# Two first products, then two second products: a reordered main stage in a three-layer kernel on one Trainium2 core

## The chip, the cores and the metric

One core of a Trainium2 chip runs the whole program. TensorE (PE) multiplies matrices, with its weight loads shown apart (PEld); VectorE (DVE), ScalarE (ACT) and GpSimd (POOL) do elementwise work; SyncE (SP) issues the transfers. The metric is the device time of one execution in microseconds, the median of three runs: 2111.48 us for the kernel before (2109.56 to 2112.36).

## The reference

Three layers on 4 x 576 = 2304 tokens of width 512. All values are float32.

```
x = attention(q, k, v, ...)                       # local softmax attention and a memory term
P = sinkhorn(exp(x @ w_gate))                     # 2304 x 8, a weight per token and expert
out = 0
for e in range(8):                                # the experts
    h = max(x @ w1[e], 0)                         # 512 -> 1024
    out += P[:, e:e+1] * (h @ w2[e])              # 1024 -> 512
h = out @ w_in                                    # the wide layer: 512 -> 2048
y = max(0.01*h, h) @ w_out                        # 2048 -> 512
```

## The kernel before

Attention, the gate and the first expert take the first 424 us. All later work is in `rest`, and the change is in its loop over `steps`. Every float32 operand there is split into a high and a low part, and a product is three matmuls: high by high, low by high, high by low.

**Steps.** The tokens go through in two passes, 1280 tokens and 1024. A pass has token groups `s`: two of 512 tokens (`s` = 0, 1), and in the first pass a third of 256 (`s` = 2). A unit `u` is 512 hidden columns: experts 1 to 7 are units 2 to 15, the wide layer is units 16 to 19. A unit's columns come in two halves, `fp` = 0 and 1. The segments are: experts on the first pass (84 steps), experts on the second (56), the wide layer on the first (24) and on the second (16). The order is unit, group, half.

**One step.** `l1(st)` computes the half's hidden values: 42 matmuls of 256 columns into four PSUM banks `pq` (a Strassen-like scheme of seven products, `PRODUCTS`), or 24 into one bank for `s` = 2. After the first bank, ACT copies a part of it (`s`, L918) and six DVE operations (L920 to L925) put the sums into `c`; then `half(0)` and `half(1)` each make the high part `hh` on ACT (L931) and the low part `hl` on DVE (L932). `l2(st)` multiplies `hh` and `hl` by the second weights into four banks `po`: 24 matmuls of 512 columns, the last of them cut into two of 256 (12 for `s` = 2). After the second half, DVE adds `po` times the token's weight to `acc` (L971).

**Pipeline.** Each turn of the loop calls `l1` of step k and then `l2` of step k-1, so PE alternates first and second products. `tc.manual_schedule()` keeps each engine's instructions in the order of the code.

**Work on the side.** In `l1`, right after the copy `s`, `pay()` calls `W.advance()` and one turn of a generator `side`:

- `W` stages weights into three slots; step (u, fp) uses instance number `inst`, and slot `inst % 3`. Each instance has two stages. Stage 0 splits the first half of `w1` (ACT copies, then POOL subtractions, L677) and makes sums on POOL (L689 to L692). Stage 1 splits those sums, the operand `s` of four of the seven products, and then `w2`. A stage may run when the products that read the slot's old content have been issued; `W.finish(inst)` at the head of `l1` runs on the spot what is missing of its instance.
- `side` builds operands for later segments: loads, ACT copies, POOL subtractions (`stl`, L735, and four sums L740 to L743).
- `conv.advance(n)` turns the wide layer's float64 weights into float32 in steps: two DVE operations a step (L804 to L813), then one POOL addition `wb` (L814) per piece.

`put_by` holds back the stores of a finished group's `acc` to the next turn.

Of the kernel before, what the change touches and what calls it, by code (L numbers as in the profile page):

```python
# [15 lines left out]
AF = mybir.ActivationFunctionType  # L16
# [4 lines left out]
P = 128  # L21
B, H, S, D = 4, 8, 576, 64
NT, DM, E, F, G = 2304, 512, 8, 1024, 2048
# [621 lines left out]
SB = 256  # L645
# [3 lines left out]
class Pairs:  # L649
# [23 lines left out]
    keep = staticmethod(lambda one: one)  # L673
# [149 lines left out]
def rest(tc, pools, W, X, xd, Pm, ident, keep, out, conv):  # L823
# [3 lines left out]
    nc = tc.nc  # L827
# [4 lines left out]
    acc = [ap.tile([P, DM], F32, name=f"acc{t}") for t in range(10)]  # L832
    kept = {(seg, s): {part: dr.tile([P, 7 * 2 * SB], F32, name=f"k{part}{seg}{s}") for part in "hl"} for seg in (1, 2, 3) for s in range(2)}
    segs = [dict(n=n, bases=PASSES[n % 2], units=range(2, 16) if n < 2 else range(16, 20)) for n in range(4)]
    steps = []
# [10 lines left out]
    def tiles(st):  # L846

        seg, s = st[0], st[2]
        T = SB if s == 2 else 2 * SB
        return T, range(4 * s, 4 * s + T // P), seg["bases"][0] // P  # L850
# [97 lines left out]
    def l2(st):  # L948
        seg, u, s, fp, inst = st
        w = W.finish(inst)  # L950
        hh, hl = hs.pop(st[1:])
        T, ts, t0 = tiles(st)
        banks = (2, 3, 0, 1) if s == 1 and fp == 1 and 2 in range(len(seg["bases"])) else tuple(range(T // P)) if s < 2 else (2, 3)
        if fp == 0:
            for j in banks:
                po[j] = pp.tile([P, DM], F32, tag=f"po{j}", name=f"po{j}")
        for f in range(2):
            for j in banks:
                r = slice(j % (T // P) * P, (j % (T // P) + 1) * P)
                for n, (a, part) in enumerate(((hh, "h"), (hh, "l"), (hl, "h"))):  # L960
                    for d in (slice(0, SB), slice(SB, DM)) if f and n == 2 and j == banks[-1] else (slice(0, DM),):
                        nc.tensor.matmul(po[j][:, d], a[:, f, r], w[1, part][:, f, d], start=(fp == 0 and f == 0 and n == 0), stop=(fp == 1 and f == 1 and n == 2 and d.stop == DM))  # L962
        if last_of[inst] is st:
            W.gone.add((inst, 1))
        if fp == 0:
            return
        e = u // 2
        for j in banks:
            t = ts[j % len(ts)]
            if u < 16:  # L970
                nc.vector.scalar_tensor_tensor(out=acc[t], in0=po[j], scalar=Pm[:, t0 + t, e:e + 1], in1=acc[t], op0=ALU.mult, op1=ALU.add)  # L971
            elif u == 16:
                nc.scalar.activation(acc[t], po[j], AF.Copy)
            else:
                nc.vector.tensor_add(acc[t], po[j], acc[t])
            if u == 19:
                nc.sync.dma_start(out=out[(t0 + t) * P:(t0 + t + 1) * P, :], in_=acc[t])
# [17 lines left out]
    def plain_from_x():  # L995
        xs = from_dram(nc, ap, xd, PASSES[0][2], P)
        at_tail["x"] = True
        yield
        for n, x in enumerate(xs):
            r = slice(n * P, (n + 1) * P)  # L1000
            nc.scalar.activation(xp["h"][:, :, r], x, AF.Copy)
            nc.vector.tensor_sub(xp["l"][:, :, r], x, f32(xp["h"][:, :, r]))
        yield

    def second_half():

        for s, t0 in enumerate(PASSES[1]):
            for n in range(2):
                xa, xb = from_dram(nc, ap, xd, t0 + n * P, SB)
                yield  # L1010
                yield from staged(1, s, n, xa, xb)
# [15 lines left out]
    def next_layer(n):  # L1027

        t0 = PASSES[n][0] // P
        rounds = [(s, j) for s in range(2) for j in range(2)]  # L1030
        of = [(t0 + 4 * s + j, t0 + 4 * s + 2 + j) for s, j in rounds]
        if n == 0:
            of.append((t0 + 8, t0 + 9))
        ts = loaded(*of.pop(0))
        yield
        at_tail["x"] = True
        yield
        for s, j in rounds:
            xs = []
            for k, a in enumerate(ts):  # L1040
                x = ap.tile([P, 4, P], F32, tag=f"x{'ab'[k]}", name=f"x{'ab'[k]}", bufs=1)
                nc.scalar.activation(x, turned(a), AF.Copy)
                xs.append(x)
            yield
            ts = loaded(*of.pop(0)) if of else ()
            for k, _ in enumerate(staged(n + 2, s, j, *xs)):
                if k == 2:
                    if n == 0:
                        yield
                    if of or ts:  # L1050
                        at_tail["x"] = True
                yield
        if n == 0:
            for k, a in enumerate(ts):
                r = slice(k * P, (k + 1) * P)
                ps = turned(a)
                nc.scalar.activation(xp["h"][:, :, r], ps, AF.Copy)
                nc.vector.tensor_sub(xp["l"][:, :, r], ps, f32(xp["h"][:, :, r]))
            yield

    def side(n):

        if n == 0:
            yield from plain_from_x()
            yield from second_half()
        elif n < 3:
            yield
            yield
            yield from next_layer(n - 1)

    more = owed = None
    at_tail = {}
    sides = []
    put_by = []
    for k, st in enumerate(steps):
        seg, u, s, fp, inst = st
        if more is None or seg is not steps[k - 1][0]:
            more = side(seg["n"])
            sides.append(more)
        for t in put_by:  # L1080
            nc.sync.dma_start(out=keep[t * P:(t + 1) * P, :], in_=acc[t - seg_t0])
        put_by = []
        last_half = l1(st)
        turn = [more]
        last = steps[k - 1] if k else None
        behind = k and (last[2] == 2 and last[3] == 1 or u >= 16)
        if last_half and not behind:
            last_half()
        if k:
            l2(last)  # L1090
            if behind and at_tail.pop("x", None):
                next(turn.pop(), None)
            if last_half and behind:
                last_half()
            if last[1] == 15 and last[3] == 1:
                _, ts, seg_t0 = tiles(last)
                put_by = [seg_t0 + t for t in ts]
        if u == 2 and fp == 1:
            _, ts, t0 = tiles(st)
            for t in ts:  # L1100
                nc.scalar.activation(acc[t], acc[t], AF.Copy, scale=Pm[:, t0 + t, 0:1])
        if at_tail.pop("x", None):
            next(turn.pop(), None)
        owed = turn
        if seg["n"] < 2:
            conv.advance(1 + (k % 2 if seg["n"] == 0 else 1))
    l2(steps[-1])
    assert all(next(one, None) is None for one in sides) and next(conv.todo, None) is None

# [4 lines left out]
def body(tc, qt, kt, qn, vn, zn, beta, M_prev, w_gate, w1, w2, w_in, w_out, out):  # L1114
    nc = tc.nc
    with ExitStack() as ctx:
# [138 lines left out]
        with right, ExitStack() as rx:  # L1255
            pool = lambda name, bufs=1, **kw: rx.enter_context(tc.tile_pool(name=name, bufs=bufs, reuse_waits="tile", **kw))
            ap, hp_, conv_ = pool("r_acc"), pool("r_h"), pool("r_conv")
            pq, pp = pool("r_pq", 4, space=PSUM), pool("r_po", space=PSUM)
            conv = Convert(tc, conv_, w_in, w_out, *wide)
            with tc.manual_schedule():  # L1260
                rest(tc, (ap, hp_, pq, pp, dr), WR, X, xd, Pm, ident, keep, out, conv)
# [39 lines left out]
```

## Time and profile before

| | |
|---|---|
| median of three runs | 2111.48 us |
| profiled execution, its own time | 2110.44 us |
| its span in the trace | 2108.6 us |
| PE busy | 2091.1 us, 99% of the span |
| DVE, POOL, ACT busy | 66%, 53%, 36% |
| chain that ended last: PE | 94% |
| granted TensorE clock | 1.0 throughout |

The span is the traced execution from its first to its last instruction. The chain that ended last follows the program back from its last instruction to what released each one. PE's line numbers are L911 (first products), L897 (first products of `s` = 2) and L962 (second products).

### The profile page before, as it was taken

The numbers are of one execution on the slowest core, as the hardware profiler recorded it, in microseconds if no ns is written. First come the engines' busy times: TensorE is split into PE (matmuls) and PEld (weight loads), VectorE is DVE, ScalarE is ACT, GpSimd is POOL, SyncE is SP. The second block draws the span as 40 slices with busy tenths as digits, with TensorE's granted clock in tenths as the row PEclk, the third lists the DMA queues.
The fourth block names the chain that finished last, engine by engine and source line by source line (L and its number), as shares of the span: only waits on it lengthen the run. The fifth ranks groups of instructions, "written<-read, shape, count | busy, mean of one in ns | idle before, by whom it ended". The sixth has DMA issues, their size and how long they took to land.

```text
span 2108.6 us, 35243 instructions
## 1 busy us (share of the span) xinstructions
PE 2091.1 (99%) x13845; PEld 1853.6 (88%) x13845; DVE 1393.3 (66%) x2507; ACT 764.1 (36%) x1575; POOL 1116.9 (53%) x1011
## 2 busy tenths in 40 slices
PE   8899999999999999999999999999999999999999
PEld 5677778999999999999999999999999999999998
DVE  7766557366766666666666788666666665666676
ACT  7766643343332222222222433332323324333331
POOL 4522223556755444554444678775555554665651
PEclk9999999999999999999999999999999999999999
DMA  6544312354422222212227343421111161337111
GB/s 198 179 125 123 114 55 81 100 170 145 131 84 68 65 71 71 76 65 66 71 71 286 103 146 96 127 70 60 51 50 61 41 240 61 110 99 262 42 60 40
DMA packets 164422, 217.81 MB, mean 103 GB/s; under 512 B 13984, under 2 KB 109216, under 8 KB 162720
## 3 DMA queue, kind: packets, MB, share of 16 engines
q1 hardware_dynamic: 164256, 215.55, 31.7%
q8 instruction: 109, 1.79, 0.3%
q14 instruction: 57, 0.47, 0.1%
HBM read 166.23 MB, written 49.28 MB: 102 GB/s over the span
## 4 chain that ended last, share of the span: by engine, by line
PE 94%; DVE 2%; ACT 1%; POOL 1%; DMA 1%; issue 0%; SPq 0%; DVEq 0%; ACTq 0%; POOLq 0%
PE po L962 42%; PE pq L911 33%; PE pq L897 5%; PE ph L561 4%; PE po L569 4%; PE avps L313 2%; PE sps L252 1%; PE atps L287 1%; PE avps L310 1%; PE sps L246 1%; DVE a L263 1%; DMA nq<-in_qn_dram 1%; ACT a L265 1%; PE gps L410 0%; PE xt L1024 0%; DMA raw<-in_moe_w_dram 0%
## 5 line engine op out<-in xcount | busy, mean ns | idle before, releaser
L962 PE MATMUL po<-w,hh 128*128 128x512 f32 x2592 | 799.9, 390 | 0.0
L962 PEld LDWEIGHTS po<-w,hh 128*128 128x128 f32 x2592 | 473.3, 188 | 89.0
L962 PE MATMUL po<-w,hl 128*128 128x512 f32 (+1 forms) x1476 | 506.1, 363 | 0.0
L677 POOL TENSOR_TENSOR w0l<-raw,w0h 128x512 fp32r<-128x512 f32 x144 | 185.6, 1311 | 276.2 <-ACT w0h L676 276.2
L962 PEld LDWEIGHTS po<-w,hl 128*128 128x128 f32 x1476 | 276.9, 188 | 58.3
L932 DVE SCALAR_TENSOR_TENSOR hl<-c,hh 128x512 fp32r<-128x512 f32 x224 | 245.6, 1131 | 80.0 <-ACT hh L931 80.0
L911 PE MATMUL pq<-Xh,w0h 128*128 128x256 f32 x960 | 266.7, 278 | 0.0
L911 PE MATMUL pq<-Xl,w0h 128*128 128x256 f32 x960 | 265.7, 277 | 0.0
L911 PE MATMUL pq<-Xh,w0l 128*128 128x256 f32 x960 | 265.4, 276 | 0.0
L918 ACT ACTIVATE s<-pq 128x256 f32<-128x256 f32 x144 | 55.1, 383 | 489.9 <-PE pq L911 489.8
L677 POOL TENSOR_TENSOR w<-raw,w 128x512 fp32r<-128x512 f32 x144 | 217.6, 1533 | 0.0
L931 ACT ACTIVATE hh<-c 128x512 fp32r<-128x512 f32 x224 | 129.1, 624 | 232.0 <-DVE c L925 232.0
L971 DVE SCALAR_TENSOR_TENSOR acc<-po,Pm,acc 128x512 f32<-128x512 f32 x252 | 173.2, 740 | 29.7 <-PE po L962 28.4
L911 PEld LDWEIGHTS pq<-Xl,w0h 128*128 128x128 f32 x960 | 180.7, 188 | 0.0
L911 PEld LDWEIGHTS pq<-Xh,w0l 128*128 128x128 f32 x960 | 180.4, 188 | 0.0
L911 PEld LDWEIGHTS pq<-Xh,w0h 128*128 128x128 f32 x960 | 180.2, 188 | 0.0
L920 DVE TENSOR_TENSOR uv<-pq,s 128x256 f32<-128x256 f32 x144 | 60.7, 421 | 163.0 <-ACT s L918 162.8
L814 POOL TENSOR_TENSOR wb<-wa,wc 128x512 f32<-128x512 f32 x32 | 41.3, 1292 | 155.5 <-DVE wc L813 111.0
L677 POOL TENSOR_TENSOR ql<-raw,qh 128x512 fp32r<-128x512 f32 x48 | 62.3, 1319 | 90.2 <-ACT qh L676 90.2
L911 PE MATMUL pq<-Xh,w1h 128*128 128x256 f32 x384 | 106.1, 276 | 0.0
L911 PE MATMUL pq<-Xl,w1h 128*128 128x256 f32 x384 | 106.1, 276 | 0.0
L911 PE MATMUL pq<-Xh,w1l 128*128 128x256 f32 x384 | 106.1, 276 | 0.0
(266 smaller groups left out, 4842.5 us busy)
## 6 DMA issues: line engine op xcount, KB each, us to landing
raw<-in_moe_w_dram SPq DMA_DIRECT2D x136, 512.0 KB, 3.5
Xh<-kh SPq DMA_DIRECT2D x6, 1792.0 KB, 7.5
Xl<-kl SPq DMA_DIRECT2D x6, 1792.0 KB, 11.8
f<-in_moe_w_in_dram SPq DMA_DIRECT2D x16, 512.0 KB, 4.9
f<-in_moe_w_out_dram SPq DMA_DIRECT2D x16, 512.0 KB, 3.7
raw<-wide_in SPq DMA_DIRECT2D x16, 512.0 KB, 3.2
raw<-wide_out SPq DMA_DIRECT2D x16, 512.0 KB, 3.7
kh<-sth SPq DMA_DIRECT2D x12, 512.0 KB, 4.9
```

The costliest lines, as they stand in the source:

```text
L313: nc.tensor.matmul(av[j * D:(j + 1) * D, o + nq - sn:o + nq], r["v"][:, j, c, :], at[:, j, s0:s0 + sn], start=False, stop=i == len(parts) - 1)
L561: nc.tensor.matmul(ph[:, :T], wp[:, c, f0:f0 + P], x[:, c, t0:t0 + T], start=(n == 0), stop=(n == 11))
L569: nc.tensor.matmul(po, a[:, s], wp[:, c, :], start=(first and n == 0), stop=(last and n == 2))
L677: self.keep(self.nc.gpsimd.tensor_sub(lo, src, f32(hi)))
L897: nc.tensor.matmul(ph[:, f * SB:(f + 1) * SB], wp(a, c % 2), xp[x][:, c], start=(n == 0), stop=(n == 11))
L911: nc.tensor.matmul(b[-1][:, o:o + SB], wp(a, c), X[s][part][:, x, c], start=(n == 0), stop=(n == 5))
L918: nc.scalar.activation(s1, b[0][:, lo], AF.Copy)
L920: v.tensor_add(uv[:, 0], b[0][:, up], s1)
L931: nc.scalar.activation(hh[:, f], c, AF.Relu)
L932: v.scalar_tensor_tensor(out=hl[:, f], in0=c, scalar=0.0, in1=f32(hh[:, f]), op0=ALU.max, op1=ALU.subtract)
L962: nc.tensor.matmul(po[j][:, d], a[:, f, r], w[1, part][:, f, d], start=(fp == 0 and f == 0 and n == 0), stop=(fp == 1 and f == 1 and n == ...
L971: nc.vector.scalar_tensor_tensor(out=acc[t], in0=po[j], scalar=Pm[:, t0 + t, e:e + 1], in1=acc[t], op0=ALU.mult, op1=ALU.add)
```

## The change

In the two expert segments, all but the last two steps are taken in pairs of the two halves of one unit and group: both first products, then both second products. 138 of the 140 steps are in 69 pairs. In a pair's first half `pay()` only stages weights (`owed = ()`); in the second half it also turns `side`. Conversion steps follow each first product. The cut of the last second product into two of 256 columns is left out in the first half, where another second product follows. The stores of `acc` are issued right after their second products. From the last two expert steps on, the loop is the old one, and it starts with `owed = None`, so that the first of these steps stages nothing.

```diff
-                    for d in (slice(0, SB), slice(SB, DM)) if f and n == 2 and j == banks[-1] else (slice(0, DM),):
+                    for d in (slice(0, SB), slice(SB, DM)) if (fp or u >= 16) and f and n == 2 and j == banks[-1] else (slice(0, DM),):
...
-    put_by = []
-    for k, st in enumerate(steps):
-        seg, u, s, fp, inst = st
+    def store(st):
+
+        if st[1] == 15 and st[3] == 1:
+            _, ts, t0 = tiles(st)
+            for t in ts:
+                nc.sync.dma_start(out=keep[(t0 + t) * P:(t0 + t + 1) * P, :], in_=acc[t])
+
+    both = sum(1 for st in steps if st[0]["n"] < 2) - 2
+    for k in range(0, both, 2):
+        two = steps[k:k + 2]
+        seg, u = two[0][:2]
         if more is None or seg is not steps[k - 1][0]:
             more = side(seg["n"])
             sides.append(more)
-        for t in put_by:
-            nc.sync.dma_start(out=keep[t * P:(t + 1) * P, :], in_=acc[t - seg_t0])
-        put_by = []
+        for n, st in enumerate(two):
+            owed = [more] if n else ()
+            last_half = l1(st)
+            if last_half:
+                last_half()
+            conv.advance(1 + (n or seg["n"]))
+        if u == 2:
+            _, ts, t0 = tiles(st)
+            for t in ts:
+                nc.scalar.activation(acc[t], acc[t], AF.Copy, scale=Pm[:, t0 + t, 0:1])
+        for st in two:
+            l2(st)
+        if at_tail.pop("x", None):
+            next(more, None)
+        store(st)
+    owed = None
+    for k, st in enumerate(steps):
+        if k < both:
+            continue
+        seg, u, s, fp, inst = st
+        if seg is not steps[k - 1][0]:
+            more = side(seg["n"])
+            sides.append(more)
         last_half = l1(st)
         turn = [more]
-        last = steps[k - 1] if k else None
-        behind = k and (last[2] == 2 and last[3] == 1 or u >= 16)
+        behind = k > both and (u >= 16 or steps[k - 1][2] == 2 and fp == 0)
         if last_half and not behind:
             last_half()
-        if k:
-            l2(last)
+        if k > both:
+            l2(steps[k - 1])
...
-            if last[1] == 15 and last[3] == 1:
-                _, ts, seg_t0 = tiles(last)
-                put_by = [seg_t0 + t for t in ts]
-        if u == 2 and fp == 1:
-            _, ts, t0 = tiles(st)
-            for t in ts:
-                nc.scalar.activation(acc[t], acc[t], AF.Copy, scale=Pm[:, t0 + t, 0:1])
+            store(steps[k - 1])
...
         if seg["n"] < 2:
-            conv.advance(1 + (k % 2 if seg["n"] == 0 else 1))
+            conv.advance(2)
```

Three places of the order, by engine. First ACT at the start of the wide layer. `s_...` is the copy (L918) inside an `l1`, `qh` stage 0 and `sh` with `w` stage 1 of the instance that unit 16's second half uses, `hh` the two high parts of a step (L931 experts, L935 wide layer). Before:

```order
L676 ACTIVATE qh_3493<-raw_17881 128x512 x2
L931 ACTIVATE hh<-c 128x512 x2
L918 ACTIVATE s_18082<-pq 128x256
L676 ACTIVATE sh_3495<-raw_17881 128x512 x2
L676 ACTIVATE w_4247<-raw_17887 128x512 x2
L935 ACTIVATE hh<-c 128x512 x2
L918 ACTIVATE s_18191<-pq 128x256
```

And now:

```order
L918 ACTIVATE s_18004<-pq 128x256
L676 ACTIVATE qh_3493<-raw_17907 128x512 x2
L935 ACTIVATE hh<-c 128x512 x2
L676 ACTIVATE sh_3495<-raw_17907 128x512 x2
L676 ACTIVATE w_4247<-raw_17913 128x512 x2
L918 ACTIVATE s_18121<-pq 128x256
```

Stage 1 (`sh`, `w`) stood in the first products of (16, 0, 0), ahead of that step's `hh`; now stage 0 stands there, and stage 1 comes behind the `hh`, at the head of the first products that use it, those of (16, 0, 1).

Second, POOL at the end of unit 6 in the first pass. `raw` is the end of stage 0 of the instance for the next unit's second half, `stl`, `xa` and `xb` are one turn of `side`, `wb` the conversion, `w1l` the first piece of work of stage 1. Before, a turn of `side` of this kind in the first pass:

```order
L735 TENSOR_TENSOR stl<-xa,sth 128x512
L735 TENSOR_TENSOR stl<-xb,sth 128x256
L740 TENSOR_TENSOR xa<-xb,xa 128x256
L741 TENSOR_TENSOR xb<-xb 128x256
L742 TENSOR_TENSOR xb<-xb,xa 128x256
L743 TENSOR_TENSOR xa<-xb,xa 128x256
L677 TENSOR_TENSOR ql_3494<-raw_5896,qh_3493 128x512 x2
```

And now:

```order
L692 TENSOR_TENSOR raw_7162<-raw_7162 128x2x128
L735 TENSOR_TENSOR stl<-xa,sth 128x512
L735 TENSOR_TENSOR stl<-xb,sth 128x256
L740 TENSOR_TENSOR xa<-xb,xa 128x256
L741 TENSOR_TENSOR xb<-xb 128x256
L742 TENSOR_TENSOR xb<-xb,xa 128x256
L743 TENSOR_TENSOR xa<-xb,xa 128x256
L814 TENSOR_TENSOR wb<-wa,wc 128x512
L677 TENSOR_TENSOR w1l_397<-raw_7162,w1h_396 128x512 x2
```

Before, such a turn stood ahead of an instance's stage 0; now this one stands between stage 0 and stage 1 of the same instance, across the boundary of two units, with a conversion's addition behind it. The same happens at the end of unit 2, without `wb`.

Third, DVE in the first group of unit 2 in the second pass: the end of one first product's work (L925, `hl`), what follows, and the start of the next one's (L920). Before:

```order
L925 TENSOR_TENSOR c<-pq,s_12158 128x256
L932 SCALAR_TENSOR_TENSOR hl<-c,hh 128x512
L971 SCALAR_TENSOR_TENSOR acc_4736<-po_12081,Pm,acc_4736 128x512
L971 SCALAR_TENSOR_TENSOR acc_4737<-po_12082,Pm,acc_4737 128x512
L932 SCALAR_TENSOR_TENSOR hl<-c,hh 128x512
L804 TENSOR_SCALAR wc<-f_11874 128x512
L805 TENSOR_SCALAR wc<-wc 128x512
L807 SCALAR_TENSOR_TENSOR wc<-f_11874,wc 128x512
L808 TENSOR_SCALAR wa<-wc 128x512
L920 TENSOR_TENSOR uv<-pq,s_12256 128x256
```

And now:

```order
L925 TENSOR_TENSOR c<-pq,s_12133 128x256
L932 SCALAR_TENSOR_TENSOR hl<-c,hh 128x512 x2
L804 TENSOR_SCALAR wc<-f_11838 128x512
L805 TENSOR_SCALAR wc<-wc 128x512
L807 SCALAR_TENSOR_TENSOR wc<-f_11838,wc 128x512
L808 TENSOR_SCALAR wa<-wc 128x512
L920 TENSOR_TENSOR uv<-pq,s_12214 128x256
```

The four conversion operations stand between the two first products as they did; on PE the second products that lay between these two first products are no longer there.

## Rows read from the trace of the kernel before

**Rows 1.** The page: its first line, and PE's busy time.

```profile
span 2108.6 us, 35243 instructions
...
PE 2091.1 (99%) x13845; PEld 1853.6 (88%) x13845; DVE 1393.3 (66%) x2507; ACT 764.1 (36%) x1575; POOL 1116.9 (53%) x1011
```

**Rows 2.** The chain in order of time, first pass: shares by line; start, length, work.

```profile
by line: PE po L962 52.4%; PE pq L911 37.0%; PE pq L897 10.6%
...
424.29 9.80 PE pq L911 x84
...
439.55 4.78 PE pq L911 x42
444.33 5.46 PE po L962 x25
```

**Rows 3.** Timeline of PE inside a second and a first product: start, length, instruction.

```profile
1485.06 0.61 PE L962 MATMUL po<-w,hh 128*128 128x512 f32 x2
...
1485.74 0.61 PE L962 MATMUL po<-w,hh 128*128 128x512 f32 x2
...
1489.17 0.28 PE L911 MATMUL pq<-Xh,sh 128*128 128x256 f32 x1
...
1489.85 0.28 PE L911 MATMUL pq<-Xh,sh 128*128 128x256 f32 x1
```

**Rows 4.** Timelines of PE, ACT and POOL at the start of the wide layer.

```profile
1725.90 1.14 ACT L676 ACTIVATE sh<-raw 128x512 fp32r<-128x512 f32 x2
...
1726.61 2.55 POOL L677 TENSOR_TENSOR sl<-raw,sh 128x512 fp32r<-128x512 f32 x2 [3.76 <-ACT sh L676]
...
1734.23 0.29 PE L911 MATMUL pq<-Xh,qh 128*128 128x256 f32 x1
...
1735.92 0.63 ACT L935 ACTIVATE hh<-c 128x512 fp32r<-128x512 f32 x1 [4.31 <-DVE c L934]
1736.46 0.36 ACT L918 ACTIVATE s<-pq 128x256 f32<-128x256 f32 x1
```

**Rows 5.** The chain and POOL's timeline around the end of unit 3, first pass.

```profile
499.40 1.74 POOL L735 TENSOR_TENSOR stl<-xa,sth 128x512 fp32r<-128x512 f32 x1
...
504.78 0.74 POOL L743 TENSOR_TENSOR xa<-xb,xa 128x256 f32<-128x256 f32 x1
510.81 1.29 POOL L814 TENSOR_TENSOR wb<-wa,wc 128x512 f32<-128x512 f32 x1 [5.29 <-DVE wc L813]
...
511.95 2.74 PE pq L897 x24
...
515.98 2.54 POOL L677 TENSOR_TENSOR w0l<-raw,w0h 128x512 fp32r<-128x512 f32 x2 [1.40 <-ACT w0h L676]
...
521.04 0.74 POOL L692 TENSOR_TENSOR raw<-raw 128x256 f32<-128x256 f32 x1
...
528.03 2.56 POOL L677 TENSOR_TENSOR w1l<-raw,w1h 128x512 fp32r<-128x512 f32 x2 [6.25 <-ACT w1h L676]
533.15 4.78 PE pq L911 x42
```

**Rows 6.** Timelines of DVE, POOL and PE: the work behind a first product, and conversion.

```profile
430.49 1.29 DVE L932 SCALAR_TENSOR_TENSOR hl<-c,hh 128x512 fp32r<-128x512 f32 x2 [0.70 <-ACT hh L931]
...
1159.48 0.42 DVE L920 TENSOR_TENSOR uv<-pq,s 128x256 f32<-128x256 f32 x1
...
1161.93 0.42 DVE L925 TENSOR_TENSOR c<-pq,s 128x256 f32<-128x256 f32 x1
1163.05 2.90 DVE L932 SCALAR_TENSOR_TENSOR hl<-c,hh 128x512 fp32r<-128x512 f32 x2 [0.70 <-ACT hh L931]
...
1206.31 0.95 DVE L804 TENSOR_SCALAR wc<-f 128x512 int32<-128x512 int32 x1
...
1208.49 0.43 DVE L808 TENSOR_SCALAR wa<-wc 128x512 int32<-128x512 int32 x1
...
1703.51 0.29 PE L911 MATMUL pq<-Xh,qh 128*128 128x256 f32 x1
1706.13 2.56 POOL L677 TENSOR_TENSOR w1l<-raw,w1h 128x512 fp32r<-128x512 f32 x2 [3.76 <-ACT w1h L676]
...
1709.61 2.57 DVE L932 SCALAR_TENSOR_TENSOR hl<-c,hh 128x512 fp32r<-128x512 f32 x2 [0.70 <-ACT hh L931]
```

## The prediction

> **What bounds the kernel now.** I read the page first: the span is 2108.6 us, and PE is busy for 2091.1 us of it [rows 1]. Then the chain of work that ended last, in order of time, because a busy PE says nothing of who waits. From 424.29 us to the end of the first pass its shares by line are 52.4, 37.0 and 10.6%, all of them PE, and no other engine and no wait appears in it [rows 2]. So in the stretch that the change touches PE is dense, and everything else lies beside it. Two things follow. The change can gain only what PE itself pays, which is the price of alternating between products of 256 and 512 columns. And it can lose wherever it shortens the PE work that covers another engine's chain.
>
> **What PE pays for alternating.** Within a second product, three matmuls of 512 columns take 1485.74 - 1485.06 = 0.68 us, so 0.2267 us each; within a first product six of 256 columns take 1489.85 - 1489.17 = 0.68 us, so 0.1133 us each [rows 3]. A step at these rates is 42 x 0.1133 + 24 x 0.2267 = 4.76 + 5.44 = 10.20 us. The chain shows 4.78 + 5.46 = 10.24 us [rows 2]. So one round from first to second product and back costs 0.04 us, the cut of the last matmul included. A pair goes round once where two steps went round twice: 69 pairs x 0.04 = **2.8 us gained**. That is also the ceiling: nothing else on PE changes. The program already has one place where two first products follow each other, at the start: 84 matmuls in 9.80 us against 84 x 0.1133 = 9.52 us [rows 2], and the 0.28 us is no more than a start. I take it that the join of two first products is free; if it cost the whole 0.28 us, 69 of them would take 19 us, and that is a far upper end which I leave out of the sum, because those first matmuls follow a change of stage.
>
> **What the cover was.** Between a first product and the second product that uses it stood a second and another first product, 10.2 us. In a pair the first half has 4.76 us (the other first product), the second half 5.44 us (the first half's second product). I go through what is queued in these spans, engine by engine.
>
> *PSUM.* Each first product needs all four banks `pq`, so the second half writes the banks that DVE is still reading of the first half. The first bank is read a third of the way through its own product and written again 4.76 us later, and DVE keeps up with the product: the first `hl` starts at 1709.61 us, 1.3 us after the end of a product that began at 1703.51 us, so all six additions are done by then [rows 6]. I cost this at nothing. If DVE were 3 us late, PE would wait there.
>
> *The wide layer's start (ACT, POOL).* The new loop's first step stages nothing, so every later stage comes one step late, until `finish` runs one on the spot: stage 1 for (16, 0, 1) at the head of that very product. The seventh matmul of the product needs `sh`, the ninth `sl`, and the order shows both behind the wide layer's `hh`. Before, `sh` was copied at 1725.90 us, long ahead. The product starts at 1734.23 us; its ninth matmul is due 8 x 0.1133 later, at 1735.14 us. ACT finishes the `hh` that it now has to do first and takes its next instruction at 1736.46 us; `sl` starts 1726.61 - 1725.90 = 0.71 us after `sh` and takes half of 2.55 us, so it ends at 1738.45 us [rows 4]. With the time of one matmul, 0.11 us, for loading the weights, PE waits **3.4 us**. Nothing hides it, since the operand is needed at once; the second piece of `sl` ends 1.28 us later, and PE reaches it then. Lower end 2.2 us (only `sh` counts), upper end 4.7 us (one more POOL piece of 1.28 us ahead of it).
>
> *Unit boundaries, first pass (POOL).* The slot of unit u's first half is refilled for the next unit's second half: stage 0 after the first product of (u, 2, 0), stage 1 in the next unit's first product. In the row where this can be seen, (u, 2, 0) ends at 511.95 + 2.74 = 514.69 us, and POOL ends stage 0 at 521.04 + 0.74 = 521.78 us, 7.1 us later. PE then needs the first `sl` piece at the ninth matmul of the first product at 533.15 us, 18.5 + 0.9 = 19.4 us after 514.69 [rows 5]. In the new order PE has 2.72 + 5.44 + 0.04 + 4.76 = 12.96 us up to that product, so 13.9 us. POOL without other work is early: its stage 1 would start as soon as ACT's copy is there. But at the end of unit 2 a turn of `side` stands between, 505.52 - 499.40 = 6.1 us: 7.1 + 6.1 + 1.3 = 14.5 us, **0.6 us late**. At the end of unit 6 the conversion's addition of 1.3 us stands there as well [rows 5]: 15.8 us, **1.9 us late**. The other boundaries have the shorter kind of turn or none, and are in time. Sum 2.5 us, lower end nothing (POOL's rows vary by over 1 us with what DVE does), upper end 5 us.
>
> *Second pass, while conversion lasts (DVE).* Take a pair's start as zero. The first half's `hl` pair ends at 1709.61 + 2.57 - 1703.51 = 8.7 us with POOL's stage 1 beside it. Then come the conversion operations that the order shows between the two first products. Four of them take 1208.49 + 0.43 - 1206.31 = 2.6 us: 11.3 us. The six additions take 1161.93 + 0.42 - 1159.48 = 2.9 us: 14.15 us. `hl` follows 1163.05 - 1162.35 = 0.7 us later, and its first piece takes 0.65 to 1.45 us: it ends at 15.5 to 16.3 us [rows 6]. PE wants it at the third matmul of the second half's second product: 2 x 4.76 + 0.02 + 5.44 + 2 x 0.2267 = 15.43 us. So up to 0.9 us late; POOL has a stage 0 to do at that time, so I take 0.7 us. In the order five pairs of the second pass have three or four operations there: three with four, 0.7 us each, and two with three, where an operation of about 0.65 us fewer leaves 0.2 us. Sum **2.5 us**. In the first pass at most two operations stand there, and DVE is about 1 us early. Lower end nothing. Upper end: if the `hl` of the first half took 2.90 us and the conversion doubled as `hl` does, each of the five would be 3 to 4 us late, 17 us in all.
>
> What bears on the last term is the Trainium skill, page "SBUF — State Buffer", section "Who interferes with whom": a DVE instruction with two inputs in SBUF contends with a GpSimd instruction that reads SBUF. The trace agrees in kind: two `hl` take 1.29 us at 430.49 us, when POOL was idle, and 2.57 to 2.90 us beside POOL [rows 6]. Without that effect the DVE term would be nothing, and the sum 2.5 us less.
>
> *At nothing:* the stores that come earlier on SP's queue (they wait for `acc`, and the loads behind them wait for POOL's stage 1, which ends later); the scaling of `acc`, which has a whole second product before it is used; the skipped stage in the first half, which only moves `side` to every other step.
>
> **The sum.** 2110.4 us for the profiled execution, less 2.8, plus 3.4, 2.5 and 2.5, is 2110.4 + 5.6 = **2116.0 us**. That execution lies 1.0 us under the median of 2111.48 us, within the spread of the three runs.
>
> **Rivals.**
> - *The added work on POOL and DVE stays covered; only the wide layer's start waits.* The margins that I call missed are 0.6, 1.9 and 0.2 to 0.9 us, and a POOL or DVE row that is 20% shorter closes most of them. 2110.4 - 2.8 + 3.4 = 2111.0 us: no change. Against it speaks that `hl` beside POOL is always slow.
> - *Nothing waits anywhere*, not even at (16, 0, 1): 2110.4 - 2.8 = 2107.6 us, a gain below what can be told. It decides at one point: whether PE's ninth matmul there waits for POOL. For it speaks nothing in the rows.
> - *DVE becomes the bound of pairs.* If conversion beside POOL doubles, the DVE term is around 9 us instead of 2.5, half of its upper end: 2122.5 us. For it speaks the 2.90 us row; against it, that POOL has a pause between its two stages in which the first operations run.
>
> **Chances.** My sum, with 3 to 9 us added, 0.50; only the start of the wide layer 0.30; nothing waits 0.07; DVE the bound 0.13. A difference of 0.2% is 4.2 us, about what a measurement of this kernel can tell from no change. Of my own case four parts in five lie above it, so slower is 0.40 + 0.13 = 0.53; faster by over 4.2 us would need more than the ceiling of 2.8 us, 0.02; the rest, 0.45, is the same. The range goes from 2109.5 (just under the second case) to 2122 us, which leaves out nothing-waits and most of the last case; my own case alone is 2113.5 to 2119.5 us.
>
> **What would show it.** In the changed profile, a pair in the chain should read 4.78, 4.76, 5.44 and 5.46 us, 20.44 us in place of 20.48. PE should have one wait of about 3.4 us in the first product of (16, 0, 1), released by POOL `sl`; about 0.6 and 1.9 us released by POOL at the ends of units 2 and 6; and five short waits on DVE `hl` at the start of the second pass. I am wrong if the pair does not get shorter, if PE waits at the join of two first products for DVE, or if those waits are missing.

## The result

The changed kernel takes 2130.15 us (median of 5 runs, 2128.57 to 2131.24); the kernel before took 2110.89 us on the same chip. The ratio is 1.0091, with a 95% interval from 1.0080 to 1.0102: slower, by 19.3 us where I had forecast 5.6. The profiled execution has a span of 2128.8 us, 20.2 us more than in [rows 1]. Its page, first line and busy times:

```profile
span 2128.8 us, 35032 instructions
...
PE 2099.4 (99%) x13775; PEld 1854.2 (87%) x13775; DVE 1430.7 (67%) x2507; ACT 761.6 (36%) x1575; POOL 1121.5 (53%) x1011
```

PE is busy for 8.3 us more, with 70 matmuls fewer. Some matmuls must have become slower. DVE is busy for 37 us more with the same 2507 instructions. The chain in order of time answers to [rows 2]: start, length, work.

```profile
656.07 9.54 PE pq L911 x84
665.61 10.90 PE po L962 x49
```

A pair takes 9.54 + 10.90 = 20.44 us, as forecast, and here the join of two first products is free (84 x 0.1133 = 9.52). So the loss lies elsewhere. The view of what PE waited for, from 424 us to the end (total, times, longest); in the kernel before this view has no row at all:

```profile
PE po L962 <- ACT hh L931: 5.3, 5, 2.2
PE pq L911 <- POOL w1l L677: 2.6, 1, 2.6
PE pq L911 <- ACT sh L676: 1.9, 1, 1.9
PE pq L911 <- POOL sl L677: 1.7, 2, 0.9
PE po L962 <- DVE hl L932: 0.5, 1, 0.5
PE pq L911 <- DVE uv L920: 0.4, 1, 0.4
```

These sum to 12.4 us. More is visible in the view by windows (the busy time of PE, PEld, DVE, ACT and POOL, then the granted clock, the DMA's share and GB/s) around three of the waits:

```profile
695.80:700.00 4.20, 4.20 (x25) 4.20 (x26) 1.58 (x4) 0.39 (x1) 4.02 (x3) 0.66 0.33 106
...
1173.40:1176.00 2.60, 0.38 (x2) 0.20 (x2) 0.22 (x1) 1.92 (x4) 1.21 (x1) 1.00 0.19 68
1176.00:1180.00 4.00, 3.87 (x10) 2.76 (x10) 3.97 (x4) 2.72 (x5) 3.84 (x4) 0.57 0.00 0
1180.00:1184.00 4.00, 4.00 (x23) 3.40 (x22) 3.88 (x6) 0.00 (x0) 3.14 (x4) 1.00 0.00 0
...
1753.00:1757.00 4.00, 3.15 (x16) 3.15 (x16) 0.42 (x1) 1.39 (x3) 4.00 (x4) 0.57 0.22 71
```

Behind each of these waits PE runs for some 4 us at a granted clock of 0.57 to 0.66, which is mostly its lower level of 1.2 GHz. From 1176 us it has 10 matmuls in 4 us and counts as busy. That is part of why busy time rose, and of why the sum of waits is too small; the other part is that each wait in this view begins only at the modelled end of the matmul before it.

**The wide layer's start**, which answers to [rows 4] (timelines of ACT, PE and POOL):

```profile
1751.30 0.63 ACT L935 ACTIVATE hh<-c 128x512 fp32r<-128x512 f32 x1 [4.76 <-DVE c L934]
1751.84 1.13 ACT L676 ACTIVATE sh<-raw 128x512 fp32r<-128x512 f32 x2
...
1752.50 0.39 PE L911 MATMUL pq<-Xh,sh 128*128 128x256 f32 x1 [1.93 <-ACT sh L676]
...
1752.53 2.51 POOL L677 TENSOR_TENSOR sl<-raw,sh 128x512 fp32r<-128x512 f32 x2 [4.10 <-ACT sh L676]
```

The copy `sh` stands behind `hh`, as the prediction said, and PE waits for both pieces. By the starts of its matmuls, less their usual spacing, it loses 2.08 us at 1752.5 and 1.01 us at 1753.9 us, with a smaller gap 3.36 us in all. Waits are given in this way from here on; the view of waits, which counts idle time alone, puts each a little lower.

**The end of unit 6**, which answers to [rows 5] (timeline of POOL):

```profile
680.54 2.99 POOL L677 TENSOR_TENSOR w0l<-raw,w0h 128x512 fp32r<-128x512 f32 x2 [13.98 <-ACT w0h L676]
...
687.60 1.29 POOL L735 TENSOR_TENSOR stl<-xa,sth 128x512 fp32r<-128x512 f32 x1
...
692.71 1.27 POOL L814 TENSOR_TENSOR wb<-wa,wc 128x512 f32<-128x512 f32 x1
693.93 3.40 POOL L677 TENSOR_TENSOR w1l<-raw,w1h 128x512 fp32r<-128x512 f32 x2
```

Stage 0, the operands' step, the conversion's addition and stage 1 follow each other without a pause, in the order forecast. Two rows are longer than I had put them: 2.99 and 3.40 us instead of 2.54 and 2.56 (of the second, PE needs only the first of two pieces). PE waits 3.0 us at 695.7 us, and 1.2 us in the same way at the end of unit 2 (484.5 us).

**DVE in the second pass**, which answers to [rows 6] (timeline of DVE, then of PE):

```profile
1254.14 0.68 DVE L807 SCALAR_TENSOR_TENSOR wc<-f,wc 128x512 int32<-128x512 int32 x1
1254.85 1.57 DVE L808 TENSOR_SCALAR wa<-wc 128x512 int32<-128x512 int32 x1
1256.46 1.67 DVE L810 SCALAR_TENSOR_TENSOR wa<-wc,wa 128x512 int32<-128x512 int32 x1
1258.16 0.84 DVE L811 TENSOR_SCALAR wb<-wa 128x512 int32<-128x512 int32 x1
...
1262.50 0.73 PE L962 MATMUL po<-w,hh 128*128 128x512 f32 x2 [1.80 <-ACT hh L931]
```

Four conversion operations take from 1254.14 to 1259.00, 4.9 us instead of 2.6. POOL works beside them from 1254.84 us on (stage 0). What follows on DVE is late, so ACT's `hh` and the second product are late too. The kernel before has such rows, earlier in its trace than those that I read: there the four operations that I priced at 2.6 us stand at 442 us beside a subtraction on POOL (from 442.49 us), and take 445.86 + 1.40 - 442.26 = 5.0 us.

```profile
442.26 0.42 DVE L804 TENSOR_SCALAR wc<-f 128x512 int32<-128x512 int32 x1
442.72 1.40 DVE L805 TENSOR_SCALAR wc<-wc 128x512 f32<-128x512 f32 x1
...
445.86 1.40 DVE L808 TENSOR_SCALAR wa<-wc 128x512 int32<-128x512 int32 x1
```

In both traces, no conversion operation on DVE takes more than 0.69 us while POOL is idle; with POOL at work throughout they take up to 1.80 us.

**The start of the second pass**, which the prediction had at nothing (timelines of SP's DMA queue and of ACT):

```profile
1159.70 0.32 SPq L815 DMA_DIRECT2D wide_out<-wb  x1
...
1160.59 0.89 SPq L1079 DMA_DIRECT2D keep<-acc  x2
1161.53 6.01 SPq L876 DMA_DIRECT2D acc<-keep  x8
1167.91 1.05 SPq L669 DMA_DIRECT2D raw<-in_moe_w_dram  x2
...
1174.08 1.15 ACT L676 ACTIVATE qh<-raw 128x512 fp32r<-128x512 f32 x2 [8.73 <-DMA raw<-in_moe_w_dram]
1175.14 1.14 ACT L931 ACTIVATE hh<-c 128x512 fp32r<-128x512 f32 x2
```

ACT stands for 8.73 us before the copy `qh`, and the `hh` that PE needs is queued behind that copy and starts at 1175.14 us. The same place in the kernel before:

```profile
1150.13 4.11 SPq L876 DMA_DIRECT2D acc<-keep  x8
1154.62 2.38 SPq L669 DMA_DIRECT2D raw<-in_moe_w_dram  x2
1157.09 0.89 SPq L1081 DMA_DIRECT2D keep<-acc  x2
...
1160.98 1.15 ACT L676 ACTIVATE qh<-raw 128x512 fp32r<-128x512 f32 x2 [2.93 <-DMA raw<-in_moe_w_dram]
```

The same copy `s` of the pass's first product starts at 1150.09 us before and at 1160.01 us after. Counted from it, the raw loads issue at 4.5 us before and at 7.9 us after, because two stores stand ahead (0.9 us), the eight loads take 6.01 us to issue instead of 4.11 (why, no run here shows), and the conversion's store above them comes 0.5 us later.

### The profile page after: what moved, and what is told of

The parts are those of the page before. It is cut to its first block, busy times and chain, and to the rows that moved or that the text cites. A ratio compares the mean times of both kernels' runs of the same rounds, so it can differ in the third digit from the quotient of the medians.

```text
span 2128.8 us, 35032 instructions
## 1 busy us (share of the span) xinstructions
PE 2099.4 (99%) x13775; PEld 1854.2 (87%) x13775; DVE 1430.7 (67%) x2507; ACT 761.6 (36%) x1575; POOL 1121.5 (53%) x1011
## 4 chain that ended last, share of the span: by engine, by line
PE 87%; DVE 5%; DMA 3%; POOL 2%; ACT 2%; issue 1%; SPq 0%; POOLq 0%; DVEq 0%; ACTq 0%
PE po L962 39%; PE pq L911 30%; PE pq L897 4%; PE ph L561 4%; PE po L569 3%; PE avps L313 2%; DMA raw<-in_moe_w_dram 1%; PE sps L252 1%; PE atps L287 1%; PE avps L310 1%; DMA nq<-in_qn_dram 1%; PE sps L246 1%; ACT a L265 1%; DVE a L263 1%; DVE hl L932 1%
## 5 line engine op out<-in xcount | busy, mean ns | idle before, releaser
L962 PEld LDWEIGHTS po<-w,hh 128*128 128x128 f32 x2592 | 478.8, 188 | 100.7 <-ACT hh L931 7.4
L677 POOL TENSOR_TENSOR w0l<-raw,w0h 128x512 fp32r<-128x512 f32 x144 | 190.2, 1342 | 266.8 <-ACT w0h L676 266.8
L962 PEld LDWEIGHTS po<-w,hl 128*128 128x128 f32 x1406 | 264.3, 188 | 58.1 <-DVE hl L932 2.8
L932 DVE SCALAR_TENSOR_TENSOR hl<-c,hh 128x512 fp32r<-128x512 f32 x224 | 251.7, 1163 | 84.9 <-ACT hh L931 84.9
L911 PE MATMUL pq<-Xh,w0h 128*128 128x256 f32 x960 | 266.6, 278 | 0.4 <-DVE uv L920 0.4
L911 PE MATMUL pq<-Xl,w0h 128*128 128x256 f32 x960 | 265.7, 277 | 0.0
L911 PE MATMUL pq<-Xh,w0l 128*128 128x256 f32 x960 | 265.5, 277 | 0.0
L931 ACT ACTIVATE hh<-c 128x512 fp32r<-128x512 f32 x224 | 129.2, 624 | 233.1 <-DVE c L925 233.1
L918 ACT ACTIVATE s<-pq 128x256 f32<-128x256 f32 x144 | 54.1, 376 | 427.3 <-PE pq L911 427.3
L911 PEld LDWEIGHTS pq<-Xh,w0h 128*128 128x128 f32 x960 | 180.2, 188 | 0.8 <-DVE uv L920 0.6
L911 PEld LDWEIGHTS pq<-Xl,w0h 128*128 128x128 f32 x960 | 180.7, 188 | 0.0
L911 PEld LDWEIGHTS pq<-Xh,w0l 128*128 128x128 f32 x960 | 180.3, 188 | 0.0
L920 DVE TENSOR_TENSOR uv<-pq,s 128x256 f32<-128x256 f32 x144 | 60.3, 419 | 79.5 <-ACT s L918 79.4
L677 POOL TENSOR_TENSOR w1l<-raw,w1h 128x512 fp32r<-128x512 f32 x48 | 62.2, 1318 | 97.7 <-ACT w1h L676 97.6
L911 PE MATMUL pq<-Xh,w1l 128*128 128x256 f32 x384 | 106.9, 278 | 2.6 <-POOL w1l L677 2.6
L911 PE MATMUL pq<-Xh,sl 128*128 128x256 f32 x384 | 107.2, 279 | 1.8 <-POOL sl L677 1.7
```

Source lines behind the costliest of these rows:

```text
L677: self.keep(self.nc.gpsimd.tensor_sub(lo, src, f32(hi)))
L911: nc.tensor.matmul(b[-1][:, o:o + SB], wp(a, c), X[s][part][:, x, c], start=(n == 0), stop=(n == 5))
L918: nc.scalar.activation(s1, b[0][:, lo], AF.Copy)
L920: v.tensor_add(uv[:, 0], b[0][:, up], s1)
L931: nc.scalar.activation(hh[:, f], c, AF.Relu)
L932: v.scalar_tensor_tensor(out=hl[:, f], in0=c, scalar=0.0, in1=f32(hh[:, f]), op0=ALU.max, op1=ALU.subtract)
```

## The experiments

To place a gain I compare when the same instruction starts in two executions: ACT's copy `s`, of which each has 144. I call these marks. Where the difference between two executions jumps, time was won or lost. A constant offset from the untouched stretch ahead of the main stage (up to 1.3 us) drops out. Each place is read from one execution, and what the granted clock does behind a wait changes from one execution to the next, by up to 1.6 us in these runs. The times given first below are medians.

**The stage in the first unpaired step given back.**

```diff
-    owed = None
+    owed = ()
     for k, st in enumerate(steps):
         if k < both:
```

> The changed kernel, with one thing undone: the first unpaired step, (15,1,0) of the second pass, issues the stage of the next expert's weights that it issued in the kernel before. Theory: the wide layer's start is late because that stage is missing, and PE's 3.36 us of waits at 1752.5 and 1753.9 us are followed by about 4 us at a granted clock of 0.57 that cost another 1.5 us; both go, so the time falls by about 4.9 us against the changed kernel (2130.2 to about 2125.3), and the rows from 1748 to 1761 us show a granted clock of 1.00. Rival one: the clock's fall has nothing to do with the wait, and only 3.4 us come back (2126.8). Rival two: the stage is late for another reason (its load or ACT), and nothing comes back.

2126.38 us, ratio to the kernel before 1.0072 (1.0059 to 1.0086). The waits for `sh` and for the second `sl` are gone, the granted clock is 1.00 throughout 1744 to 1756 us, and the marks jump by 4.71 us there, more than the 3.36 us of waiting. The time alone, 3.8 us less, would not decide between the theory (4.9) and rival one (3.4); the jump and the granted clock do, for the theory.

**The kernel before, less that one stage** (its loop with `owed = None` before the step (15,1,0)).

> The kernel before, with one thing taken over from the change: in the step (15,1,0) of the second pass no stage of the next expert's weights and no operands' step is issued. Theory: the missing stage alone makes the wide layer's start late; PE waits about 3.4 us for ACT's sh and POOL's sl and then runs some 4 us at a lower granted clock, so the time rises by about 4.9 us against the kernel before (2110.9 to about 2115.8). Rival one: in the unpaired order a second product stands between, and hides the later stage: less than 1.5 us slower. Rival two: the wait comes, the clock stays at 1.00: 3.4 us slower.

2116.22 us, ratio 1.0025 (1.0014 to 1.0035). PE's waits, and the window behind them:

```profile
PE pq L911 <- ACT sh L676: 1.9, 1, 1.9
PE pq L911 <- POOL sl L677: 0.8, 1, 0.8
...
1738.00:1742.00 4.00, 3.15 (x17) 2.95 (x17) 0.42 (x1) 1.61 (x4) 4.00 (x4) 0.69 0.14 43
```

The marks jump by 4.93 us. The missing stage alone, without any pairing, makes this wait and the lower clock behind it. Both rivals fall.

**Accumulators stored one pair later** (`store` called behind the next pair's first products).

> The changed kernel, with the stores of a finished accumulator put off by one pair, so that on SP's queue they stand behind the loads of the next pair instead of ahead of them. Theory: at the start of the second pass the loads of raw weights wait behind two stores that wait for the accumulators, ACT then blocks for 8.7 us on them, PE waits 2.4 us and runs about 4 us at a granted clock of 0.57 (about 2.0 us more); all of it goes, so the time falls by about 4.4 us (to about 2125.7). Rival one: the eight loads of accumulators (6.0 us to issue on SP) and the DMA of the raw weights (6.2 us) make them late by themselves, and less than 1.5 us comes back. Rival two: the wait goes, the clock does not, 2.4 us come back.

2132.66 us, 1.0103 (1.0089 to 1.0117): no gain. SP's queue at the start of the second pass:

```profile
1162.61 3.17 SPq L1079 DMA_DIRECT2D keep<-acc  x4
1165.82 4.73 SPq L876 DMA_DIRECT2D acc<-keep  x8
1170.93 1.14 SPq L669 DMA_DIRECT2D raw<-in_moe_w_dram  x2
```

The edit put the four stores of the pair before in place of the last two, so it was not the clean test of the stores that I meant; by the rows above they are worth 0.9 us. Rival one is nearer: the eight loads of accumulators stand ahead of the raw loads in any case. So a later run turned these round.

**Accumulators loaded behind the weights' stage** (the `load_acc` calls moved in `l1` to behind `pay()`).

> The changed kernel, with the loads of accumulators at the start of a pass issued behind the weights' stage of the same step, so that on SP's queue they stand behind the loads of raw weights. Theory, after the run in which the stores were put off: ACT's 8.7 us of wait for raw weights at the start of the second pass come from the eight loads of accumulators (6.0 us to issue) that stand ahead of the raw loads on SP's queue; with the order turned, the raw loads issue some 4 us earlier, PE's 2.4 us of wait at 1175.8 us and the stretch at a granted clock of 0.57 behind it (about 2.0 us) go, and the time falls by about 4.4 us (to about 2125.7). Rival one: SP waits anyway until POOL has read the raw tiles, the accumulators then come late, and the scaling of the accumulators on ACT holds up the next evacuation: no gain, or slower. Rival two: the transfer of the raw weights is late by itself, and nothing changes.

2126.89 us, 1.0075 (1.0062 to 1.0087). SP's queue and ACT:

```profile
1163.29 3.34 SPq L669 DMA_DIRECT2D raw<-in_moe_w_dram  x2
1166.68 4.57 SPq L876 DMA_DIRECT2D acc<-keep  x8
...
1168.43 1.15 ACT L676 ACTIVATE qh<-raw 128x512 fp32r<-128x512 f32 x2 [3.37 <-DMA raw<-in_moe_w_dram]
1171.57 1.15 ACT L931 ACTIVATE hh<-c 128x512 fp32r<-128x512 f32 x2 [1.99 <-DVE c L925]
```

Counted from the same copy `s`, the raw loads issue 4.3 us earlier, ACT's wait falls from 8.73 to 3.37 us, and `hh` now waits for DVE alone. The marks jump by 4.45 us, and the clock stays at 1.00 from 1171 to 1184 us. The order of loads on SP's queue is the lever. Of the gain, 1.3 us is lost again at the next waits for `hh` and `hl`, which the changed kernel has at 1262 us. They are as long here (the view gives 1.65 and 0.51 us, against 1.80 and 0.52), but here the granted clock falls behind them:

```profile
1258.00:1262.00 4.00, 3.49 (x10) 2.56 (x9) 3.04 (x3) 0.04 (x1) 3.77 (x5) 0.57 0.37 102
```

**The operands' step of the 256-column pairs in the first half.**

```diff
-            owed = [more] if n else ()
+            owed = [more] if n != (seg["n"] == 0 and st[2] == 2) else ()
```

> The changed kernel, with the operands' step of the 256-column pairs (s=2) of the first pass issued in the first half of the pair instead of the second, that is ahead of the weights' stage 0 on POOL instead of behind it. Theory: at the ends of units 2 and 6 POOL's queue (stage 0, operands' step, stage 1) ends 1.5 and 3.0 us too late for PE, since the operands' step starts some 2.7 us later than it could; the waits at 484.5 and 695.7 us go, with the stretch at a granted clock of 0.66 behind the second, and the time falls by about 5 to 5.7 us (to about 2125). Rival: POOL has the same work in front of the same need, slowed by DVE beside it (2.99 and 3.40 us for rows of 2.54), and the start is not what is late: less than 2 us comes back.

2124.98 us, 1.0071 (1.0058 to 1.0083). Both waits are gone. Around them the marks jump by 1.47 us (unit 2) and 4.24 us (unit 6), 5.7 us as expected. Stage 0 takes 2.99 us as before, so the late start was the main cause; the first piece of stage 1 also takes 1.30 us instead of 1.71. In the profiled execution 1.6 us is lost again at the wide layer's start. The waits there are the same to 0.02 us, but the granted clock stays low for longer behind them: 0.50 from 1750 to 1753 us and 0.71 from 1753 to 1757 us.

**All conversion after the second evacuation.**

```diff
-            conv.advance(1 + (n or seg["n"]))
+            if n:
+                conv.advance(3 + seg["n"])
```

> The changed kernel, with all conversion steps of a pair issued after its second evacuation, none between the two evacuations. Theory: PE's waits for hh and hl at 515, 727, 1262 and 1285 us (0.7 + 0.7 + 2.9 + 1.5 us) come from two to four conversion rows on DVE between the first and the second evacuation; they go, and the time falls by about 5.8 us (to about 2124.4). Rival: DVE has the same work per pair, and the steps now stand ahead of the accumulators' rows and of the next pair's first evacuation, so that the waits come back there: no gain, or up to 3 us slower.

2137.87 us, 1.0129 (1.0115 to 1.0143): slower. The marks lose in the first pass and win in the second. The two places of the loss on DVE:

```profile
451.29 0.43 DVE L804 TENSOR_SCALAR wc<-f 128x512 int32<-128x512 int32 x1 [9.36 <-DMA f<-in_moe_w_in_dram]
...
594.01 1.51 DVE L804 TENSOR_SCALAR wc<-f 128x512 int32<-128x512 int32 x1 [6.00 <-POOL wb L814]
```

Issued in one piece, the conversion waits for its own load, and once for its own addition on POOL, with everything else on DVE behind it. That is a third way, neither the theory nor the rival. But the short waits at 515 and 727 us go (0.7 us each), and so do those at 1262 and 1285 us.

**The same, in the second pass only** (`conv.advance(4 * n if seg["n"] else 1 + n)`).

> The changed kernel, with the conversion of a pair of the second pass issued whole after the second evacuation; the first pass keeps its order. Theory: what made the run with all conversion late slower is the first pass alone, where DVE waited 9.4 us for the first block's load; in the second pass the waits at 1262 and 1285 us (2.9 + 1.5 us) go without a new one, and the time falls by about 4.1 us (to about 2126). Rival: without the first pass's 11.5 us of delay the second pass meets other loads and stores, and the waits stay or move: less than 1.5 us.

2126.91 us, 1.0073 (1.0060 to 1.0085). The marks jump by 2.9 us at 1262 and by 1.5 us at 1285 us, 4.4 us in all, and PE gets no new wait in the second pass. The time falls by 3.2 us, the profiled execution's by 5.2.

**The cut of the last product, with and without pairs.** First the changed kernel with the cut in both halves again (the condition `(fp or u >= 16) and` removed):

> The changed kernel, with the last product of every second product again issued as two halves of 256 columns, in both halves of a pair, as in the kernel before; the pairing stays. Theory: the 0.04 us that a pair gains in the trace come from the halves that are no longer issued, one per pair, so that 69 pairs give 2.8 us back: the time rises by about 2.8 us (to about 2133). Rival: they come from the pairing (fewer turns between first and second products), and the time stays at 2130.2.

2131.64 us, 1.0097 (1.0084 to 1.0111). Then the kernel before without it in the first halves (the same condition added):

> The kernel before, unpaired, with the one part of the change that needs no pairing: in the first half of each expert's units the last product of a second product is issued whole, not as two halves. Theory: the 0.033 to 0.04 us per pair that the trace shows come from this alone, 70 times, so that the time falls by 2.3 to 2.8 us against the kernel before (to about 2108.3), and this is the fastest version. Rival: without the pairing the whole product ends later for what waits behind it, and the gain is under 0.5 us.

2119.48 us, 1.0041 (1.0028 to 1.0053): 9 us slower than the kernel before, which neither side expected. The chain of the paired kernel with all cuts, where two first products take 9.54 us as before:

```profile
666.14 10.94 PE po L962 x50
```

And that of the unpaired kernel with fewer cuts (x25 is a second product with the cut, and one without it ends at 649.22 us):

```profile
649.22 4.95 PE pq L911 x42
654.16 5.45 PE po L962 x25
659.61 4.78 PE pq L911 x42
```

With all cuts a pair takes 9.54 + 10.94 = 20.48 us, exactly two unpaired steps [rows 2]. So fewer rounds gain nothing by themselves, and the whole 0.04 us comes from the cut that is left out. In the unpaired kernel a first product that follows an uncut second product takes 4.95 us instead of 4.78; its matmuls start every 0.118 us instead of every 0.113. Pairs are free of this, because there an uncut product is followed by another second product: what pairing does is to make the cut unnecessary. That the paired kernel with all cuts lost only 1.5 us and not 2.8 is explained by two other places: the marks win 2.9 us at the start of the second pass, where the wait is shorter and the granted clock stays at 1.00, and lose 1.5 us at 1262 us, where it falls to 0.62 (1262 to 1266 us).

**Four repairs together** (the stage, the operands' step, the conversion of the second pass, the loads of accumulators), and then the first operands' step of the first pass earlier as well:

> The changed kernel with four repairs together: the stage in the first unpaired step, the operands' step of the 256-column pairs of the first pass in the first half, the conversion of the second pass after the second evacuation, the loads of accumulators behind the weights' stage. Theory: the four causes are separate and their gains add (by the lag of equal evacuations in the single runs 4.7 + 4.9 + 4.4 + 4.5 = 18.5 us), so the time is about 2111.7, within 0.2% of the kernel before. Rival: the loop's 20 us come from one budget, POOL's and DVE's time on the memory they share, so that a wait taken away in one place returns in the next: 2116 or more.

> The kernel with the four repairs, and the first operands' step of the first pass also in the first half of its pair, so that its loads from memory issue one first product (some 4.8 us) earlier. Theory: PE's wait of about 1 us at 450 us comes from these loads, whose late end puts the operands' rows on ACT and DVE right ahead of the next evacuation; it goes, about 1 us faster than with four repairs. Rival: the loads stand behind others on SP's queue anyway, and nothing changes.

2111.07 us, 1.0002 (0.9993 to 1.0011), and 2110.14 us, 0.9997 (0.9988 to 1.0006). PE's waits from 424 us on in the first of them (its L906 is L911 of the changed kernel):

```profile
PE pq L906 <- DVE uv L920: 1.0, 1, 1.0
PE po L962 <- ACT hh L931: 0.3, 2, 0.2
```

The four gains add up: 2130.15 - 18.5 = 2111.7 was expected. In the trace too: against the changed kernel the marks jump at the five places by 1.5, 4.2, 4.5, 4.4 and 4.7 us, 19.3 us in all, as in the single runs. The rival, a budget that moves waits elsewhere, falls. The fifth edit shows no difference that these runs can tell: the wait at 450 us goes and one of about the same size appears at 441 us, behind ACT's stage 1. No version beats the kernel before by more than these runs can tell.

## Why the prediction was wrong

The time lies above my upper end of 2122 us. The direction was right, and PE waits at each place that I named, though for DVE at two pairs instead of five. The sizes were not right, nor were two places that I had at nothing. In the table, "cost" is the jump of the marks when the cause was taken away, and for the first line the chain.

| place | forecast us | cost us | shown by |
|---|---|---|---|
| 69 pairs | -2.8 | -2.8 | chains; both runs on the cut |
| wide layer's start | 3.4 | 4.7 | stage given back; kernel before less the stage (4.9) |
| ends of units 2 and 6 | 0.6 + 1.9 | 1.5 + 4.2 | operands' step in the first half |
| DVE, second pass | 2.5 | 4.4 | conversion late, second pass only |
| start of the second pass | 0 | 4.45 | loads of accumulators behind |
| DVE, first pass | 0 | 1.4 | conversion late everywhere |

The costs sum to 17.9 us of the 20.2 us between the spans. About 2.3 us remain. By the starts of the matmuls, about 0.9 us of it is PE's wait at 450.7 us, at the join of two first products: there the second one waits for DVE (0.4 us in the view of waits), behind the operands' rows that run on ACT and DVE right ahead of an evacuation. I had named such a wait as a sign of being wrong; it comes this once. The rest I have not placed.

- **The pair** was right to 0.01 us, by luck. With all cuts a pair takes the 20.48 us of two unpaired steps, so the saving is not the round that I priced, but the cut that a pair can do without.
- **The wide layer's start.** Wait and cause were right: 3.4 forecast, 3.36 measured. What failed is a term that the sum lacks altogether: behind a wait PE can run at 1.2 GHz for some us. By rows it cost 4.71 - 3.36 = 1.35 us here and 4.24 - 3.0 = 1.2 us at the end of unit 6. At the start of the second pass 4.45 - 2.4 = 2.0 us lie behind the first wait, of which the clock can be (1 - 0.57) x 4.00 = 1.7 us. That is about 4.3 us in all. No row of the kernel before showed it, because PE never waited there. The Trainium skill, page "TensorE: Matmul & The Clock Gate", section "Part 1: The HAM clock gate (the "warmup" mystery)", says that the lower rate is the default and that activity lifts it; by that rule a wait has a second price behind it. The trace agrees where the granted clock falls to 0.57 behind the waits at 1175.8 and 1752.5 us. It doesn't fall behind each: from 1262 to 1266 us, with some 2.7 us of waiting, it is 1.00. Nor does it fall behind the same wait in each execution: with the accumulators' loads behind and with the late conversion of the second pass, PE waits the same 2.6 us for `w1l` at the end of unit 6, the granted clock stays at 1.00 to 700 us, and the marks there are 1.0 us ahead.
- **The POOL term was mis-sized**: the order of the queue was right, but at the end of unit 6 stage 0 with its four sums took 687.60 - 680.54 = 7.1 us where my rows gave 5.8, and the first piece of stage 1 took 1.7 us instead of 1.3, while the turn of `side` took 5.1 us instead of 6.1. So 15.8 us became 16.4, PE was there 0.2 us sooner, and the clock came on top.
- **The DVE term was mis-sized**: "Four of them take 1208.49 + 0.43 - 1206.31 = 2.6 us" was read where POOL was mostly idle. Beside stage 0 four take 4.9 us, and PE has two waits of 2.7 and 1.3 us there instead of five short ones. I had weighed only the page's rule on two inputs. The same section, "Who interferes with whom" of the Trainium skill's page "SBUF — State Buffer", also names `tensor_scalar` as an operation that can take the shared ports, under conditions on its operands; whether they are met no run here shows. `L808`, one input, takes 1.57 us beside POOL and 0.43 us in [rows 6]. "In the first pass DVE is about 1 us early" failed for the same reason, by 0.7 us twice.
- **"At nothing: the stores that come earlier on SP's queue (they wait for `acc`, and the loads behind them wait for POOL's stage 1, which ends later)"** was the step that failed outright. I had looked at the stores and not at the whole queue, in which the accumulators' loads stand behind them and the raw weights behind those. The raw loads issued 3.4 us later against the same work, and the second product that stood in between when ACT waited for them before (2.93 us) was no longer there. With the two kinds of loads turned round the 4.45 us are gone.

The rivals: "DVE becomes the bound", at 2122.5 us, came nearest in size, but DVE is under a third of the loss. The other two fall, since every wait that I had named came.

## What to carry to other kernels

When a reordering halves the cover in front of an operand, list every queue that feeds the operand, the DMA queue too, and follow each instruction ahead of it, also those of work that isn't moved. Price rows by the busiest neighbourhood they can land in, not by the one where they were read. In a kernel whose PE is dense, put a second price on each wait of some us: here 1.2 to 1.7 us of lower clock behind waits of 2.4 to 3.4 us, in some executions none and in one about 3 us.

## What the hardware showed that I had not expected

- The same wait had different prices: behind equal waits at the wide layer's start the lower clock cost 1.35 us in one execution and about 1.6 us more in another; behind the 2.6 us at the end of unit 6 it cost 1.2 us in one and nothing in another.
- How a second product ends sets the pace of the whole first product behind it: 42 matmuls in 4.78 us behind a cut end, 4.95 us behind an uncut one. Why, no run here shows.
